# Token weights kept whole, kernel products four channels wide, in a long-convolution kernel with one routed token

## The chip, the cores and the metric

The kernel runs on one core of a Trainium2 chip. The metric is the device time of one execution in microseconds (us). The core has five engines with queues of their own: TensorE (PE; its weight loads, PEld, overlap its products), VectorE (DVE), ScalarE (ACT), GpSimd (POOL) and SyncE (SP), which only issues transfers. Each engine takes its instructions strictly in the order in which they were written into its queue, and an instruction that has to wait holds up all that stand behind it.

## The reference, cut to what matters

```
x  = A_u                                     # 1 x 2048 x 512, bf16
xn = layernorm(x)
# A: a long convolution of each of the 512 channels
K[d, l] = Re( sum_n C[d,n] * exp(dt[d] * A[d,n] * l) * dt[d] * B[d,n] )      # n < 128, l < 2048
y  = irfft( rfft(xn padded to 4096) * rfft(K padded to 4096) )[:2048]
s  = y + xn * Dskip
# B: one token of 2048 goes through a gated feed-forward network
r   = xn @ w_r;  idx = argmax(r)
f   = (silu(xn[idx] @ w_gate) * (xn[idx] @ w_up)) @ w_down                   # 512 -> 1376 -> 512
xb  = xn;  xb[idx] += f * sigmoid(r[idx])
out = x + s * silu(xb)
```

## The kernel before, in words

The whole program is one graph of operations. A builder writes them down with the buffers that they read and write; the table `ORDER` then gives, for each engine, the numbers of its operations in the order in which they are put into its queue, and the waits between engines follow from the buffers. Buffers share memory by fixed addresses (`R1`, `R2`, `RE`, `RS_` and so on), so that a write into a buffer also waits for all readers of what lay there. Nearly every instruction is recorded by one of a few helpers, which is why the profile shows few lines: `tt` (L596, products and sums of two tensors on DVE), `act` (L591), `evac` (PSUM to memory, L624 on ACT, L625 on DVE), `mm` (L642, products on PE), `dma` (L659).

The stages, in the order of the data:

- *Norm.* The input X comes in four loads into `X0`. DVE takes statistics and normalises 16 blocks into `XN`, together with ACT. 16 transfers regroup XN into `XZN`; four more write XN to a scratch in device memory, `scr_g`.
- *Router.* 64 products of XZN with `MR` (the weights w_r spread out) give the scores of all tokens. DVE and PE take turns over small pieces (`LRT`, `SML`) until the address of the largest stands in `SMI`. POOL gathers that token's row from `scr_g` by an indirect transfer into `GX`.
- *Input transform.* `useq1`: 64 products of XZN with a Fourier matrix, evicted into `AU` (16 evictions of 1024 columns, on ACT). `useq2`: 128 products of AU with `F2A` and `F2B`, evicted into `BIG` (16 evictions), the spectrum of the input. BIG lies over X0 and XN, 32 KB of each partition.
- *Convolution kernel.* It is made in four quarters of 128 channels (`h`, `s`, in the profile's order 00, 01, 10, 11). `exps` and `sines` make 32 lags of exponentials (`E`) and sines (`SN`) for 256 channels on ACT; `cols` turns them into real and imaginary columns on DVE; `rows_` makes 20 further powers `GG` by complex products `cmul` on DVE with multipliers `MB` and scratch `TT`. `kgen_mm` multiplies both: for each channel and part one product of 128x32 by 128x20, four channels beside each other in the PE array, evicted to `KE` and spread into `KX` by a few more products.
- *Spectrum.* `spec`: 160 products of KX with the transform `FD` per quarter, evicted into `KF`; DVE multiplies them into BIG. `inv_a` multiplies BIG (and a swapped copy, made by transfers) by the first inverse matrix, evicted into `CC`.
- *Token.* The network's weights come in 27 pieces through a ring of four buffers `WRING`, each a transfer that POOL issues when the piece before it has been used. The product of gate and up and the down product are spread among the kernel products on PE. The result is added to the token's row (`GRW`), and an indirect transfer scatters it back into `scr_g`.
- *End.* `G0` (printed as G) is loaded from `scr_g`, over the memory of SN, and goes through silu on ACT in four pieces. `fin`: CC times the last inverse matrix `FB`, five blocks for each half of the channels; DVE multiplies with G into `TB`, partly after an ACT eviction `YB`, and adds X in `XR`, which is stored.

The last lines of the builder set the numbering of the operations: `exps(0)`, `sines(0)`, `rows_`, `cols`, `kgen_mm(0, 0)`, and so on to `spec(1, 1)`, `inv_a(1, 1)`, `fin(1)`.

Of the kernel before, what the change touches and what calls it, by code (L numbers as in the profile page):

```python
# [16 lines left out]
KB = 1024  # L17
# [300 lines left out]
ROWS = [0, 4, 256, 260, 512, 516, 768, 772, 1024, 1280, 1536, 1792, 2, 6, 258, 262, 1, 5, 3, 7]  # L318
# [9 lines left out]
def tables():  # L328
# [33 lines left out]
    for q in range(2):  # L362
# [17 lines left out]
        580 564 562 565 689 767 770 332 695 701-702 779 704 797 781 783 782 794 809 800 815 789-790 812 792 818 881 884 890 896 822 834 902 826 835  # L380
        820 905 836-837 907 913 864 868-869 876 915 925 927 921 930 941 943 946 934 933 949-950""",
    vector="""
        295 294 149 147 157 155 150 148 144 146 143 152 151 145 99 96 98 104 101 107 109 158 156 154 100 106 108 103 153 39 159 97 171 160 105 161
        40 162 42 163 38 164 111 165 37 166 41 167 102 168 110 169 112 170 113 172 114 173 115 124 116 179 117 174 118 177 119 176 120 178 121 44
        122 175 123 93 125 95 126 94 129 132 131 130 133 127 66 68 59 64 61 60 63 69 62 67 77-78 80 83 70 65 71 84 74 89 85 92 72-73 436-437 90
        438-439 470 445 471 440 444 203 446-447 202 453 452 441 454 443 442 529 448-449 455 450 460 472 461 451 462 456-457 463 459 496 465 469 458
        473 468 474 476 464 475 467 466 530 532 531 477 535 533 536 534 495 205 498 206 497 207 504 500 499 209 502 501 503 507 506 211 505 212 512
        213 511 214 513 508 514 510 520 519 509 522 515-516 216 617 517 619 523 527 518 218 524 219 525 220 521 221 618 528 620-621 526 626 357 627
        223 358 224 628-629 623 635 634 622 637 625 624 636 631 630 643 632-633 642 638-639 644 640 645 641 650-651 705 646 706-707 647 708-709 648
        714-715 227 717 716 649 723 711 662 722 710 724 713 725 712 664 655 652 719 718 731 720-721 668 727 730 665 674 732-733 726 671 728-729 734  # L390
        739 735 738 683 737 736 677 680 750 755 753 758 653 685 654 658 656 659 657 764 756 765 743 762 744 768 745 691 771 759 331 329-330 328 746
# [17 lines left out]
def build(nc, A_u, A_A_re, A_A_im, A_B_re, A_B_im, A_C_re, A_C_im, A_log_dt, A_Dskip,  # L409
# [51 lines left out]
    with g.ctx:  # L461
# [425 lines left out]
        for m4 in range(16):  # L887
            useq1(m4)
# [361 lines left out]
```

## Time and profile before

| | |
|---|---|
| runs shown | 194.26, 191.87, 194.05 us; median 194.05 |
| the profiled execution | 194.93 us; its span on the core 193.1 us |
| granted TensorE clock, mean | 0.867 |
| busy of the span | PE 136.7 us (71%), DVE 153.1 (79%), ACT 131.8 (68%), POOL 24.9 (13%) |
| instructions | PE 2960 products, DVE 385, ACT 258, POOL 37 |
| moved | 31.64 MB in 24849 packets |

The page gives the busy share of each engine in 40 slices of the span, the granted clock of PE (10 tenths are full speed), the waits, and the chain of work that ended last, followed back from the last instruction to whatever released it. A timeline row has start, length, engine, line, instruction, what it writes and reads, shapes, and a count where equal neighbours are put together; in brackets, the idle time before it and what ended it. In a product's row stand first the columns that are moved through the array and then the stationary operand, and the second shape is that of what is moved.

### The profile page before, as it was taken

To read this page: it belongs to the slowest core of one execution; us is meant where nothing else is said; L and a number is where in the kernel's file an instruction comes from. 1 tells how busy PE (TensorE), PEld (TensorE's weight loads), DVE (VectorE), ACT (ScalarE), POOL (GpSimd) and SP (SyncE) were. 2 spreads that over 40 slices of the span, in tenths; PEclk is the share of its full clock that TensorE was granted. 3 is DMA by queue.
4 is the path that set the end of the run, shared out by engine and by line. 5 is a ranking of instruction groups with operands and counts; after the bars stand their busy time and mean duration, and the time that the engine had idled before them with its cause. 6 is when DMAs were issued, how large, how long until landed. Compare 5 with 4: busy or idle time off the path is not lost.

```text
span 193.1 us, 6819 instructions
## 1 busy us (share of the span) xinstructions
PE 136.7 (71%) x2960; PEld 117.9 (61%) x2960; DVE 153.1 (79%) x385; ACT 131.8 (68%) x258; POOL 24.9 (13%) x37
## 2 busy tenths in 40 slices
PE   0110800096887998992899995799999999969741
PEld 0000700094555674871899995798999899958520
DVE  0979999999999899995899999187526429569972
ACT  0799999999999989987768973123224352599321
POOL 6000000000000000691134040033130100000000
PEclk9999999999669559998599999555699999987975
DMA  5996016690000009899955999058255294914465
GB/s 153 392 380 249 2 54 207 228 384 0 0 0 0 5 3 312 196 316 334 300 135 147 224 201 244 15 160 216 65 157 142 55 377 88 340 35 100 97 124 117
DMA packets 24849, 31.64 MB, mean 164 GB/s; under 512 B 11028, under 2 KB 19348, under 8 KB 24180
## 3 DMA queue, kind: packets, MB, share of 16 engines
q1 hardware_dynamic: 19438, 23.14, 40.9%
q10 hardware_dynamic: 3894, 3.84, 7.4%
q0 software_dynamic: 1488, 4.23, 7.1%
q8 instruction: 23, 0.38, 0.8%
q14 instruction: 6, 0.05, 0.1%
HBM read 20.72 MB, written 4.20 MB: 129 GB/s over the span
## 4 chain that ended last, share of the span: by engine, by line
PE 33%; DVE 30%; DMA 20%; issue 9%; ACT 4%; POOL 1%; SPq 1%; POOLq 0%; DVEq 0%
PE PB L642 33%; DMA GX<-scr_g,SMI 7%; DMA X<-in_A_u_dram 5%; DVE TT L596 5%; DMA scr_g<-GRW,SMI 4%; DMA G<-scr_g 4%; DVE SL L596 3%; DVE GG L596 3%; DVE ST L791 3%; DVE XN L815 2%; DVE MB L596 2%; DVE SN L596 2%; DVE E L596 2%; DVE TB L596 2%; ACT YB L591 1%
## 5 line engine op out<-in xcount | busy, mean ns | idle before, releaser
L642 PE MATMUL PB<-KX,FD 128*128 128x128 bf16 x640 | 42.3, 229 | 0.0
L642 PEld LDWEIGHTS PB<-KX,FD 128*128 128x128 bf16 x640 | 39.6, 104 | 0.5 <-issue 0.2
L596 DVE TENSOR_TENSOR BIG<-BIG,KF 128x1024 bf16<-128x1024 bf16 x32 | 21.5, 688 | 14.5 <-ACT KF L624 14.4
L596 DVE TENSOR_TENSOR TT<-GG,MB 128x512 bf16<-128x512 bf16 (+2 forms) x64 | 27.9, 470 | 0.0
L624 ACT ACTIVATE KF<-PB 128x512 bf16<-128x512 f32 x23 | 13.7, 594 | 20.3 <-PE PB L642 19.2
L642 PE MATMUL PB<-CB,BIG 128*128 128x128 bf16 x256 | 23.3, 257 | 2.1 <-ACT CC L624 1.7
L642 PEld LDWEIGHTS PB<-CB,BIG 128*128 128x128 bf16 x256 | 20.8, 155 | 3.0 <-DVE BIG L596 2.0
L642 PE MATMUL PB<-GG,SN 128*32 128x20 bf16 x512 | 18.8, 220 | 3.4 <-issue 3.4
L642 PEld LDWEIGHTS PB<-GG,SN 128*32 128x32 bf16 x512 | 18.0, 170 | 3.5 <-issue 3.5
L591 ACT ACTIVATE E<-AR 128x256 bf16<-128x256 f32 x62 | 20.0, 403 | 0.0
L642 PE MATMUL PB<-GG,E 128*32 128x20 bf16 x512 | 19.1, 223 | 0.4 <-DVE E L596 0.4
L642 PEld LDWEIGHTS PB<-GG,E 128*32 128x32 bf16 x512 | 17.5, 167 | 2.8 <-issue 1.8
L882 POOL DMA_INDIRECT GX<-scr_g,SMI x1 | 8.1, 8071 | 74.8 <-DVE GG L596 74.8
L596 DVE TENSOR_TENSOR GG<-TT 128x256 bf16<-128x256 bf16 (+2 forms) x66 | 17.6, 305 | 0.0
L624 ACT ACTIVATE BIG<-PB 128x1024 bf16<-128x1024 f32 x16 | 15.8, 1016 | 1.4 <-PE PB L642 1.3
L642 PE MATMUL PB<-MR,XZN 128*128 128x64 bf16 x64 | 5.9, 275 | 14.7 <-DMA XZN<-XN 14.7
L624 ACT ACTIVATE AU<-PB 128x1024 bf16<-128x1024 f32 x16 | 15.4, 1035 | 0.6 <-PE PB L642 0.6
L642 PE MATMUL PB<-CB,XZN 128*128 128x256 bf16 x64 | 13.4, 360 | 2.6 <-ACT AU L624 2.6
L642 PEld LDWEIGHTS PB<-MR,XZN 128*128 128x128 bf16 x64 | 5.8, 205 | 15.0 <-DMA XZN<-XN 15.0
L791 DVE BATCH_NORM_STATS2 ST<-X 128x6 f32<-128x512 bf16 x16 | 10.2, 675 | 5.7 <-DMA X<-in_A_u_dram 5.7
L624 ACT ACTIVATE CC<-PB 128x1024 bf16<-128x1024 f32 (+1 forms) x11 | 9.5, 878 | 6.7 <-PE PB L642 6.7
L642 PEld LDWEIGHTS PB<-CB,XZN 128*128 128x128 bf16 x64 | 8.8, 182 | 6.8 <-ACT AU L624 6.3
(128 smaller groups left out, 250.1 us busy)
## 6 DMA issues: line engine op xcount, KB each, us to landing
FD<-c_fd SPq DMA_DIRECT2D x4, 1280.0 KB, 9.5
XZN<-XN SPq DMA_DIRECT2D x16, 128.0 KB, 2.1
scr_g<-XN SPq DMA_DIRECT2D x4, 512.0 KB, 3.4
XR<-in_A_u_dram SPq DMA_DIRECT2D x4, 512.0 KB, 9.8
FB<-c_fb SPq DMA_DIRECT2D x1, 2048.0 KB, 9.1
G<-scr_g SPq DMA_DIRECT2D x2, 1024.0 KB, 8.9
BIG<-BIG ACTq DMA_DIRECT2D x3, 512.0 KB, 5.8
WRING<-in_B_w_down_dram POOLq DMA_DIRECT2D x10, 128.0 KB, 2.8
```

The costliest lines, as they stand in the source:

```text
L591: g.op(AC, lambda e: e.activation(out=out.ap, in_=in_.ap, func=func, **kw), w=[out], r=r, cost=extra + cost(AC, out, 0.834) - (20 if in_.b ...
L596: g.op(eng, lambda e: e.tensor_tensor(out=out.ap, in0=a.ap, in1=b.ap, op=op), w=[out], r=[a, b], cost=cost(eng, out, rate))
L624: g.op(AC, lambda e: e.activation(out=out.ap, in_=in_.ap, func=ACT.Copy), w=[out], r=[in_], cost=cost(AC, out, 0.834) - 20, alt=(DV, lambd ...
L642: ins = e.matmul(o_.ap, lhsT=l_.ap, rhs=r_.ap, start=st, stop=sp, **kw)
L791: g.op(DV, lambda e, b=b: e.bn_stats(ST6(ST6.a[b]).ap, X0(X0.a[b]).ap), w=[ST6(ST6.a[b])], r=[X0(X0.a[b])], cost=593)
L815: lambda e, ov=ov, iv=iv, mv_=mv_, rv=rv: e.tensor_scalar(out=ov.ap, in0=iv.ap, scalar1=mv_.ap, scalar2=rv.ap, op0=ALU.subtract, op1=ALU.m ...
L882: g.op(PO, lambda e: e.indirect_dma_start(out=GX(None, 0, 8).ap, out_offset=None, in_=rows, in_offset=bass.IndirectOffsetOnAxis(ap=SMI(Non ...
```

## The change

1. *Weights.* The ring and its 27 transfers on POOL's queue are gone. Six transfers on SP load all of w_gate, w_up and w_down at once: `WGA` (w_gate and a quarter of w_up) into the memory of X0, `WGB` into that of MR, `WGC` into the old ring, `WDN` (all of w_down) into the memory of XN. Since BIG lies over X0 and XN, every eviction of useq2 has to wait for the network's last product. The network's code stands ahead of useq1.
2. *Kernel products.* E, SN and CO are laid out by quarter, channel group and lag, GG with both parts side by side. One product takes four channels, 128 stationary columns (4 channels x 32 lags) by 80 moved ones (4 x 20); of its 4 x 4 blocks only the diagonal ones are used. A quarter has 64 of them in three pieces, each evicted to `K4`. Before it had 256 column-packed ones and one eviction.
3. *Complex products.* `cmul` makes all four partial products in one instruction where the source allows it, so three instructions instead of four. `cols` has three instructions instead of nine, and the chain that makes the multipliers uses double-width ones.
4. *Order.* A new `ORDER`, another list `ROWS` of the powers, three YB buffers, four PSUM bank pairs in the second `fin`, larger stores.

The core of the diff:

```diff
-ROWS = [0, 4, 256, 260, 512, 516, 768, 772, 1024, 1280, 1536, 1792, 2, 6, 258, 262, 1, 5, 3, 7]
+ROWS = [0, 256, 512, 768, 4, 260, 516, 772, 1024, 1280, 1536, 1792, 1, 5, 2, 6, 3, 7, 258, 262]
-        E = g.buf("E", RE, [32, 256], BF16)
-        GG = g.buf("GG", RG, [2, 20, 256], BF16)
+        E = g.buf("E", RE, [2, 4, 32, 32], BF16)
+        GG = g.buf("GG", RG, [20, 2, 256], BF16)
-        WRING = [g.buf(f"WRING{i}", RWR + 1536 * i, [768], BF16) for i in range(NWR)]
+        WGA = g.buf("WGA", R2, [5, 1376], BF16)
+        WGB = g.buf("WGB", R1 + 32 * KB, [2, 1376], BF16)
+        WGC = g.buf("WGC", RWR + 2560, [1376], BF16)
+        WDN = g.buf("WDN", R2 + 16 * KB, [11, 512], BF16)
...
+        load(WGC(), _dma_rows(B_w_up, 384 * FF, [[FF, 128], [1, FF]]), 128 * FF * 2, eng=None)
+        load(WGA(WGA.a[0:4]), rows_of(B_w_gate, 0, 4), 512 * FF * 2, eng=None)
+        load(WGA(WGA.a[4]), _dma_rows(B_w_up, 0, [[FF, 128], [1, FF]]), 128 * FF * 2, eng=None)
+        load(WGB(), rows_of(B_w_up, 1, 2), 256 * FF * 2, eng=None)
+        load(WDN(WDN.a[0:10]), _dma_rows(B_w_down, 0, [[512, 128], [65536, 10], [1, 512]]), 1280 * 1024, eng=None)
+        load(WDN(WDN.a[10], 0, 96), _dma_rows(B_w_down, 655360, [[512, 96], [1, 512]]), 96 * 1024, eng=None)
...
             sc = TT[si[0] % 2]
-            tt(DV, sc(t[0]), src, MB(bc(mr, (2, n, w))), ALU.mult)
-            tt(DV, sc(t[1]), src, MB(bc(mi, (2, n, w))), ALU.mult)
-            tt(DV, dst_r, sc(t[0, 0]), sc(t[1, 1]), ALU.subtract)
-            tt(DV, dst_i, sc(t[0, 1]), sc(t[1, 0]), ALU.add)
+            if n == 1 or src.strides[0] == 2 * src.strides[1]:
+                sv = np.lib.stride_tricks.as_strided(src, shape=(2 * n, w), strides=(src.strides[1], src.strides[2]))
+                tt(DV, sc(t.reshape(2, 2 * n, w)), GG(bc(sv[None], (2, 2 * n, w))), MB(bc(m[:, None], (2, 2 * n, w))), ALU.mult)
+            else:
+                for k in range(2):
+                    tt(DV, sc(t[k]), GG(src), MB(bc(m[k], (n, 2, w))), ALU.mult)
+            tt(DV, GG(dst[:, 0]), sc(t[0, :, 0]), sc(t[1, :, 1]), ALU.subtract)
+            tt(DV, GG(dst[:, 1]), sc(t[0, :, 1]), sc(t[1, :, 0]), ALU.add)
...
-                    for j in range(4):
-                        ch = 128 * s + 32 * j + c
-                        lst.append((bank(bank.a[o_:o_ + 20], 32 * j, 32), (E, SN)[ri]((E, SN)[ri].a[:, ch]), GG(GG.a[ri, :, ch]), ri == 0, ri == 1, (0, 32 * j)))
+            for c0, n in ((0, 6), (12, 6), (24, 4)):
+                for c in range(2 * n):
+                    for ri in range(2):
+                        gv = GG.a[:, ri, 128 * s:128 * s + 128].reshape(20, 32, 4)[:, c0 + c]
+                        lst.append((bank(bank.a[o_:o_ + 80]), (E, SN)[ri]((E, SN)[ri].a[s].reshape(128, 32)[:, c0 + c]), GG(gv), ri == 0, ri == 1, None))
+                mm(lst, 63)
+                evac(K4(K4.a.reshape(80, 32)[:, c0:c0 + 2 * n].reshape(80, 2, n)), PP[0](PP[0].a.reshape(2, 512)[:, :80 * n].reshape(2, n, 80).transpose(2, 0, 1)))
...
-                pr = PP[3 * (kb % 2) if h else 0]
+                pr = PP[(0, 3, 2, 1, 0)[kb] if h else 0]
-                    y_ = YB[kb % 2]
+                    y_ = YB[kb % 3]
```

Where the router's end stands on DVE. Before, it lies behind the third quarter's first complex products; the index SMI is row 188 of DVE's queue, with the products of the powers (GG, TT) around it:

```order
182 L596 TENSOR_TENSOR GG<-TT_109 128x2x128
183 L596 TENSOR_TENSOR TT_108<-GG,MB 128x512
184 L603 TENSOR_SCALAR SMB<-SML 64x1
185 L596 TENSOR_TENSOR TT_108<-GG,MB 128x512
186 L596 TENSOR_TENSOR SML<-PB,CF 8x1
187 L606 CAST SML<-SMB 64x1
188 L606 CAST SMI<-SML 8x1
189 L596 TENSOR_TENSOR GG<-TT_108 128x2x128 x2
```

In the changed kernel the same instructions on DVE, ahead of the first column instructions of SN and E:

```order
105 L611 TENSOR_REDUCE SML<-LRT 64x1
106 L598 TENSOR_TENSOR GG<-TT_92 128x2x128
107 L598 TENSOR_TENSOR GG<-TT_91 128x4x128
108 L598 TENSOR_TENSOR SML<-PB,CF 8x1
109 L598 TENSOR_TENSOR GG<-TT_91 128x4x128
110 L608 CAST SMI<-SML 8x1
111 L598 TENSOR_TENSOR TT_92<-GG,MB 128x1024
112 L605 TENSOR_SCALAR SN<-SN 128x4x480
```

SMI has moved from row 188 to row 110, ahead of the work on SN and E and of the third quarter's powers.

On PE, in the changed kernel, between the input transform's first products (CB,XZN) and its second ones (AU,F2A) stand the products of the gathered row (GX) and all of the network's gate and up products:

```order
15 L644 MATMUL PB<-CB,XZN 128x256 x24
16 L644 MATMUL PB<-CB,GX 64x4 x2
17 L644 MATMUL PB<-CB,XZN 128x256 x4
18 L644 MATMUL PB<-SMB,CB 128x32
19 L644 MATMUL PB<-SMB,WGA 128x1 x10
20 L644 MATMUL PB<-SMB,WGA 96x1
...
36 L644 MATMUL PB<-SMB,WGC 96x1
37 L644 MATMUL PB<-SMB,CB 128x32
38 L644 MATMUL PB<-AU,F2A 128x4x64 x16
39 L644 MATMUL PB<-GG,E 128x80
```

Before, at that place on PE, the first products ran through and the kernel products followed them; GX's two products came only after all second transforms:

```order
4 L642 MATMUL PB<-CB,XZN 128x256 x8
5 L642 MATMUL PB<-LRT,CF 64x32
6 L642 MATMUL PB<-CB,XZN 128x256 x56
7 L642 MATMUL PB<-GG,E 32x20 x4
8 L642 MATMUL PB<-GG,SN 32x20 x4
```

So the wait for GX has moved to behind 52 of the 64 first products, and 12 of these, the network and all that follows stand behind it.

The silus of G on ACT, among the evictions KF and CC. Before:

```order
144 L624 ACTIVATE CC<-PB 128x128x8
145 L591 ACTIVATE G_132<-G_132 128x2048
146 L624 ACTIVATE KF_123<-PB 128x512
147 L624 ACTIVATE CC<-PB 128x128x8
148 L591 ACTIVATE G_132<-G_132 128x2048
149 L624 ACTIVATE CC<-PB 128x128x4
150 L624 ACTIVATE CC<-PB 128x128x8
151 L591 ACTIVATE G_132<-G_132 128x2048 x2
```

In the changed kernel:

```order
143 L626 ACTIVATE KX_103<-PB 128x640
144 L626 ACTIVATE KF_106<-PB 128x512
145 L593 ACT_TABLE_LOAD
146 L593 ACTIVATE G_114<-G_114 128x2048 x4
147 L626 ACTIVATE KF_107<-PB 128x512
148 L626 ACTIVATE CC<-PB 128x128x8
```

All four silus now stand together, right behind the first spectrum eviction of the last quarter.

More of the change, by code (lines that the diff above doesn't have):

```diff
@@ new lines, in build @@
+        g.stage = "ffn"
+        todo = [(wi, dc) for wi in range(2) for dc in range(4)]
+        for k, (wi, dc) in enumerate(todo):
+            wb, wa = wv(wi, dc)
+            lst = [(fv(0, 32), CB(cb("IDB")), gu, True, False, None)] if k == 0 else []
+            for fc in range(11):
+                Mf = 128 if fc < 10 else 96
+                lst.append((fv(16 * wi + fc, 1, 0, Mf), wb(wa[128 * fc:128 * fc + Mf]), SMB(SMB.a[16 + dc:17 + dc]), False, False, None))
+            if k == 7:
+                lst.append((fv(0, 32), CB(cb("IDB")), gu, False, True, None))
+            mm(lst, 30)
@@ new lines, in build @@
+        for wi in range(2):
+            cp(DV, SMB(SMB.a[32 + 16 * wi:42 + 16 * wi]), fv(16 * wi, 10))
+            cp(DV, SMB(SMB.a[42 + 16 * wi:43 + 16 * wi], 0, 96), fv(10 + 16 * wi, 1, 0, 96))
+        act(SMB(SMB.a[64:75]), SMB(SMB.a[32:43]), ACT.Silu, table="silu")
+        tt(DV, SMB(SMB.a[80:91]), SMB(SMB.a[64:75]), SMB(SMB.a[48:59]), ALU.mult)
+        lst = [(fv(32, 4), CB(cb("IDB")), SMB(SMB.a[104:108]), True, False, None)]
+        for fc in range(11):
+            Kf = 128 if fc < 10 else 96
+            for dc in range(4):
+                lst.append((fv(32 + dc, 1), WDN(WDN.a[fc, 128 * dc:128 * dc + 128], 0, Kf), SMB(SMB.a[80 + fc:81 + fc], 0, Kf), False, False, None))
+            if fc in (3, 7):
+                mm(lst, 32)
+                lst = []
@@ new lines, in build @@
+        lst.append((fv(32, 4), CB(cb("IDB")), SMB(SMB.a[104:108]), False, True, None))
+        mm(lst, 32)
+        act(sml(6, 0, 64), sml(2, 0, 64), ACT.Tanh, scale=0.5, table="silu")
+        ts(DV, SMB(SMB.a[100:101], 0, 64), sml(6, 0, 64), 0.5, 0.5, ALU.mult, ALU.add)
+        cp(DV, sml(7, 0, 64), SMB(SMB.a[100:101], 0, 64))
+        cp(DV, SMB(SMB.a[108:112]), fv(32, 4))
+        mm([(fv(40, 128, 0, 4), SMB(SMB.a[108:112]), CB(cb("IDB")), True, True, None)], 100)
+        four = lambda t: t(None, 0, 4)
@@ new lines, in build @@
+        cp(DV, four(UPD), fv(40, 128, 0, 4))
+        ts(DV, four(UPD), four(UPD), sml(7, 0, 4), None, ALU.mult)
+        dma(GRW(None, 0, 8).ap, bass.AP(tensor=UPD.handle, offset=0, ap=[[UPD.row, 4], [64, 2], [1, 64]]), 1024, w=[GRW(None, 0, 8)], r=[UPD(None, 0, 4)])
+        tt(DV, GRW(None, 0, 8), GRW(None, 0, 8), GX(None, 0, 8), ALU.add)
+        g.op(PO, lambda e: e.indirect_dma_start(out=rows, out_offset=bass.IndirectOffsetOnAxis(ap=SMI(None, 0, 8).ap, axis=0), in_=GRW(None, 0, 8).ap, in_offset=None),
+             r=[GRW(None, 0, 8), SMI(None, 0, 8)], cost=950, dma=16 * KB, tokr=[f"scrg{a}" for a in range(4)], tokw=["row"])
@@ L1143, in build @@
-        dma(GRW(None, 0, 8).ap, bass.AP(tensor=UPD.handle, offset=0, ap=[[UPD.row, 4], [64, 2], [1, 64]]), 1024, w=[GRW(None, 0, 8)], r=[UPD(None, 0, 4)])
-        tt(DV, GRW(None, 0, 8), GRW(None, 0, 8), GX(None, 0, 8), ALU.add)
-        g.op(PO, lambda e: e.indirect_dma_start(out=rows, out_offset=bass.IndirectOffsetOnAxis(ap=SMI(None, 0, 8).ap, axis=0), in_=GRW(None, 0, 8).ap, in_offset=None),
-             r=[GRW(None, 0, 8), SMI(None, 0, 8)], cost=950, dma=16 * KB, tokr=[f"scrg{a}" for a in range(4)], tokw=["row"])
+                if kb in SEND[h]:
+                    q0, qn = SEND[h][kb]
+                    for p_ in range(4):
+                        store(_dma_rows(out, 16384 * (p_ // 2) + 512 * q0 + 256 * (p_ % 2) + 128 * h, [[32768, 32], [512, qn], [1, 128]]), XR(XR.a[q0:q0 + qn, 128 * h:128 * h + 128], 32 * p_, 32), 32 * 256 * qn, eng=None)
```

273 lines of the change are left out of this document (107 added, 166 removed), and 4 rows, old and new, of the table scalar.

## The prediction

> **What bounds the kernel now.** I read the busy digits of the page first: 40 slices of 4.83 us for each engine, the granted TensorE clock, and the DMA engines.
>
> ```profile
> PE   0110800096887998992899995799999999969741
> DVE  0979999999999899995899999187526429569972
> ACT  0799999999999989987768973123224352599321
> PEclk9999999999669559998599999555699999987975
> DMA  5996016690000009899955999058255294914465
> ```
>
> DVE is full from 10 to about 118 us, PE from about 63 to 182. ACT leaves its full stretch at about 108. So there are two regimes, a vector half and a TensorE half, and neither engine works in the other's. The stretches in numbers (columns: length; PE, PEld, DVE, ACT, POOL busy with counts; clock; DMA share; GB/s):
>
> ```profile
> 11.86:46.30 34.44, 12.39 (x92) 10.85 (x92) 34.44 (x106) 33.80 (x87) 0.00 (x0) 1.00 0.50 187
> 46.30:62.20 15.90, 11.83 (x62) 7.68 (x62) 15.81 (x42) 15.34 (x20) 0.00 (x0) 0.79 0.00 0
> 62.20:92.40 30.20, 24.70 (x692) 18.14 (x692) 26.35 (x95) 26.84 (x52) 8.66 (x3) 0.80 0.64 195
> 92.40:118.60 26.20, 26.13 (x519) 25.27 (x520) 25.55 (x57) 20.74 (x52) 6.45 (x12) 0.91 0.90 199
> 118.60:138.80 20.20, 17.02 (x322) 15.72 (x321) 12.78 (x21) 4.37 (x7) 4.26 (x8) 0.58 0.51 137
> 138.80:152.50 13.70, 13.69 (x425) 13.23 (x424) 6.85 (x13) 4.11 (x6) 1.67 (x4) 1.00 0.40 107
> 152.50:168.00 15.50, 15.41 (x271) 14.25 (x271) 8.39 (x16) 7.17 (x11) 0.85 (x1) 1.00 0.73 243
> 168.00:180.00 12.00, 9.71 (x306) 8.82 (x303) 9.37 (x12) 11.16 (x10) 0.00 (x0) 0.86 0.32 86
> 180.00:193.10 13.10, 5.20 (x296) 3.62 (x294) 8.16 (x14) 2.64 (x3) 0.00 (x0) 0.73 0.60 123
> ```
>
> The chain that ended last names what each stretch waits for (start, length, what):
>
> ```profile
> 62.18 11.31 PE PB L642 x299
> ...
> 78.96 13.44 DMA GX<-scr_g,SMI
> 92.39 0.04 issue
> 92.44 26.13 PE PB L642 x518
> 118.57 3.21 issue
> 121.78 18.59 PE PB L642 x382
> ...
> 142.36 9.78 issue
> 152.14 0.28 POOLq L292
> 152.43 8.11 DMA scr_g<-GRW,SMI
> 160.55 6.96 DMA G<-scr_g
> ...
> 189.92 0.42 DVE XR L596
> ```
>
> After 118.6 the vector engines wait for TensorE, which loses time twice: it stands 3.21 us in "issue", and from 122 to 138.8 it is granted about half the clock. Then the token's path closes the chain: its row can be scattered only at 152.43, the gate G returns at 167.5, and the silus of G fall where the last products need them.
>
> **The front end.** Prices (start, length, instruction, idle before):
>
> ```profile
> 26.43 10.32 SPq L659 DMA_DIRECT2D XZN<-XN  x16
> 38.27 5.89 PE L642 MATMUL PB<-MR,XZN 128*128 128x64 bf16 x64 [14.66 <-DMA XZN<-XN]
> 78.50 0.14 DVE L606 CAST SMI<-SML 8x1 int32<-8x1 f32 x1
> 78.96 8.07 POOL L882 DMA_INDIRECT GX<-scr_g,SMI  x1 [74.84 <-DVE GG L596]
> 64.80 1.01 ACT L624 ACTIVATE BIG<-PB 128x1024 bf16<-128x1024 f32 x1
> 115.18 1.22 DVE L596 TENSOR_TENSOR E<-E,CO 128x1024 bf16<-128x1024 bf16 x2
> 134.97 1.23 DVE L596 TENSOR_TENSOR E<-E,CO 128x2048 bf16<-128x2048 bf16 x1
> ```
>
> A 1024-element bf16 product takes 0.6 us, a 2048-element one 1.15: merging instructions saves only some 0.05 each. Adding up DVE's instructions in both orders at these prices, DVE has 2.6 us less ahead of the last XN, 25 us less ahead of SMI, 0.6 us more ahead of the last column instruction of the third quarter, and 3 us less ahead of that of the fourth. So XN ends 2.6 us sooner. SP issues 14 XZN transfers where it issued 16 of 0.645 us, the other two go through ACT, so it keeps up and the router's 64 matmuls start near 35.6. SMI comes at about 51 (bounds 48, if few of the row products ahead of it delay it, and 58).
>
> The gather then takes POOL 8.07 us, plus what it took from there to landing: 13.44 in all, under the DMA share of 0.64. The scatter's 8.11 is the lower bound. I take 12.1, so GX lands near 63.1 (59 to 71). Here the change adds its **new wait**. PE's queue reaches the gather after 52 of the 64 first-transform matmuls, near 58; behind it stand the other 12, all gate and up products, all second transforms. ACT's AU evictions and then DVE run dry near 59.5. Each microsecond that GX lands later is one for all three. I charge 3.6 us (0 to 12).
>
> The big weight loads need SP to issue six transfers behind XZN, into a stretch in which the DMA share is 0.00 (46.3 to 62.2): they are hidden there. What they cost if that cover is gone: as the new second wait, BIG overlays WGA and WDN, and so no second-transform eviction can begin before the down product. After the gather come 88 gate and up and 44 down products and a silu, about 8.7 us together, so the first BIG eviction moves from 64.8 to about 72. ACT has column and exponential work ahead of it meanwhile, and DVE its row products, so I price the delay at nothing beyond the 3.6; if their queues drain, up to 7.
>
> Before, DVE went from the last XN (31.0) to the third quarter's last E (116.4) in 85.4 us, of which it idled 3.85 + 0.65 in the two windows from 62.2 to 118.6: 80.9 of work. In the new order that piece is 3.2 longer (0.6 more in all, 2.6 less ahead of it): 84.1. I drop the 4.5 of idle time and put the 3.6 in its place: 28.4 + 84.1 + 3.6 = 116.1. **Gain 0.3**: the vector half is as long as before, with the FFN now inside it.
>
> **Kernel matmuls.** A group of four column-packed products, and larger ones with a strided or plain stationary operand:
>
> ```profile
> 62.34 0.23 PE L642 MATMUL PB<-GG,E 128*32 128x20 bf16 x4
> 62.41 0.24 PE L642 MATMUL PB<-GG,SN 128*32 128x20 bf16 x4
> ...
> 103.48 0.59 PE L642 MATMUL PB<-SMB,WRING 128*128 128x1 bf16 x17
> 103.93 1.28 PE L642 MATMUL PB<-KX,FD 128*128 128x128 bf16 x20
> ...
> 155.37 1.21 PE L642 MATMUL PB<-CB,BIG 128*128 128x128 bf16 x16
> 156.42 3.51 PE L642 MATMUL PB<-KX,FD 128*128 128x128 bf16 x60
> ```
>
> Four packed products start every 67 ns: 1024 cost 17.1 us. The new 256 load 128 columns at a stride of 32 elements, as CB,BIG does: 16 start in 1.05 us, 65.6 ns each, so 256 cost 16.8. **Even.** The bounds: 26.5 ns (17 WRING products in 0.45 us, plain loads, one column moved) and 92 (MR,XZN: 64 in 5.89, stride 64), so −10 to +6.8 us over four quarters; half of it lies after mm10 on the path. A quarter now has three evictions instead of one:
>
> ```profile
> L624 ACT ACTIVATE KE<-PB 128x640 bf16<-128x640 f32 x4 | 2.8, 702 | 8.5 <-PE PB L642 8.5
> ```
>
> At 702 ns for 640 columns, two of 960 and one of 640 cost about 2.5, 1.8 more a quarter; ACT is idle from 118 on, so nothing for the last two; in the first two, 3.6 us of ACT beside a DVE-bound stretch.
>
> [...]
>
> **TensorE half.** From the third quarter's last E to the end of the fourth quarter's products took 116.4 to 152.4 = 36.0 us before. In the new order that stretch holds 128 kernel products (8.4), 88 of CB,BIG (5.8), 80 of KX,FD at 58.5 ns (4.7) and 1.5 of small ones: 20.4. The FFN's products are gone from it, 60 KX,FD move behind it, the fetch stall and the half clock are for now left out. **Gain 15.6.** The end, 136.5, needs the fourth quarter's columns from DVE; by its sum they come near 126 (before 136.2), so they do not bind.
>
> Behind it to the first final product: 240 KX,FD (14.0), 48 CB,BIG (3.1) and 1.6, so 18.7; before 15.1. **Loss 3.6**, the moved products.
>
> The tail from there to the last XR was 167.5 to 190.3 = 22.8. Four silus of G stand in it:
>
> ```profile
> 167.53 1.92 ACT L591 ACTIVATE G<-G 128x2048 bf16<-128x2048 bf16 x1 [1.77 <-DMA G<-scr_g]
> ```
>
> 7.3 us of an ACT that was busy 11.16 of 12. Now the row is scattered long before, and G's load waits only for SN's buffer, free after the last kernel product at 136.5; landing takes about 8 (G 7.0 on the chain), so the silus run to 152, beside spectrum products. Then the first half of the tail is DVE's 9.4, and the last half, with three YB buffers and four bank pairs in turn, DVE's five products and sums of 5.2 with one YB eviction behind: 6.5. Together 15.9. **Gain 6.9.** What is late next is the spectrum's ACT evictions behind the four silus: if DVE does not take them, up to 7.
>
> Sum: 194.93 (the span 193.1 and 1.83 around it) − 0.3 − 15.6 + 3.6 − 6.9 = 175.7. To that I add clock and fetch losses. Before, 16.8 us at a clock of 0.50 to 0.53 cost at most 8.2, and the stall 3.2. The change removes no cause that I can name, and its waits are different; I put 4.3 of the 11.4 back, over a third: **180**. The profiled run is 0.9 above the median of 194.05, less than my rounding.
>
> [...]
>
> **The rivals.**
> - *The losses come along* (0.20). The order is right, but the half clock and the stall return in full, 7.1 over my 4.3: 187, from 185 to 190. For it: the clock dropped in four separate places. Against: PE has fewer distinct groups.
> - *Everything fits* (0.09). GX lands by 59.5, the clock stays full: 175.7 − 3.6 = 172 (169 to 174).
> - *No change* (0.06). The change doesn't do what it says: BIG's wait for the down product puts ACT 4 us behind, new stationary loads cost 92 ns (+3.4 on the path), G's load is held up behind SP's 4 BIG transfers so the silus stay in the tail (+6.9): 180 + 14 = 194, from 190 to 198.
> - *Slower* (0.05). PE at half clock from mm10 on. It then has 20.4 + 18.7 + 9 = 48 us of work, and 48 more at 0.50 would give 176 + 48 = 224; it decides from 22 us of extra wall time, that is, a good 40 us at half clock. Before, 16.8 us of such clock is the longest seen. I put 198 to 212 there.
>
> **How the numbers follow.** Likeliest 180 with 0.60, own range 174 to 185. With a bound of 2% (190.2 and 197.9; about what the measurement can tell): faster holds 0.60 + 0.20 + 0.09, less a little of the second: 0.86; same 0.09; slower 0.05. The range runs from 169 to 190 and leaves out the last two rivals.
>
> **What would show it.** Right: GX issued near 51 and PE waiting for it 3 to 5 us; the first BIG eviction near 72; 128-column kernel products every 66 ns; E of the fourth quarter done near 126; the scatter long before 100 and the silus of G over before 155. Wrong: kernel products near 92 ns, GX landing after 68, DVE idling between 70 and 116, or TensorE at a granted clock near 0.5 for more than 10 us after 116.

## The result and the profile after

| | before | after |
|---|---|---|
| median of the runs | 193.78 us (191.87 to 194.26) | 180.24 us (179.82 to 181.75) |
| ratio, 95% interval | | 0.933 (0.925 to 0.942) |
| the profiled execution; its span | 194.93; 193.1 us | 181.75; 179.9 us |
| granted TensorE clock, mean | 0.867 | 0.970 |
| busy: PE, DVE, ACT, POOL | 136.7, 153.1, 131.8, 24.9 us | 129.2, 149.4, 139.8, 12.4 us |
| products on PE, instructions on DVE | 2960, 385 | 2192, 329 |

The forecast was 180.0 us (169 to 190). The median lies 0.2 above it, the profiled execution, on which the sum is made, 1.8. Some terms of the sum were off by more than that, with both signs. Some executions of a kernel are slower than the rest (the kernel before took 190.65 to 197.56 us in 16 of them); the medians count them, the ratios do not, and the profiled execution of the kernel before (194.93) is one of them.

First the busy digits of the kernel after, 40 slices of 4.5 us (a row for each engine, then the granted clock of TensorE):

```profile
PE   0100035296968399999985789999999999999240
DVE  0899999999999488999999899899643599679831
ACT  0799889999999377999999859998645399964430
PEclk9999999999999999999998899999999999999965
```

Three things stand out against the rows of before. The full stretch of PE in the second half is shorter. The 5s in the row of the clock between 116 and 140 us are gone. And PE, DVE and ACT dip together in the fourteenth slice (3, 4 and 3), from 58.5 to 63 us: that is the new wait for the gathered row.

The same stretches in numbers, cut at the prediction's own marks: the router's first product, the first BIG eviction, the third quarter's last E, the fourth quarter's last kernel product, the first final product, the last XR (start and end, length; PE, PEld, DVE, ACT, POOL busy with counts; clock; DMA share; GB/s):

```profile
34.82:60.00 25.18, 20.96 (x128) 14.62 (x128) 25.00 (x57) 24.35 (x43) 7.87 (x1) 1.00 0.62 219
60.00:72.88 12.88, 10.65 (x193) 9.40 (x194) 8.83 (x25) 8.24 (x19) 1.12 (x1) 1.00 0.01 2
72.88:117.90 45.02, 40.85 (x621) 35.52 (x620) 43.09 (x96) 41.96 (x86) 2.13 (x2) 0.96 0.67 187
117.90:137.70 19.80, 19.80 (x322) 19.06 (x320) 13.86 (x18) 13.58 (x19) 0.72 (x1) 1.00 0.81 165
137.70:156.30 18.60, 18.60 (x315) 17.39 (x314) 14.36 (x26) 14.26 (x14) 0.00 (x0) 1.00 0.65 228
156.30:176.07 19.77, 13.14 (x602) 11.35 (x600) 14.79 (x22) 9.60 (x11) 0.00 (x0) 0.91 0.41 84
```

Up to 117.9 DVE is the full engine, apart from 60 to 72.9, where it idles 4 us. From 117.9 to 156.3 PE has no idle time at all, at full clock: 38.4 us of pure product time where before 51.1 (116.4 to 167.5) passed, with a stall of 3.21 us and 16.8 us at a clock of 0.50 to 0.53 among them.

Then the chain that ended last (start, length, what):

```profile
52.13 10.06 DMA GX<-scr_g,SMI
...
92.51 11.52 DMA FD<-c_fd
104.16 59.77 PE PB L644 x1165
...
166.29 0.81 issue
...
168.38 2.99 issue
```

The gather stands in it with 10.06 us, and at the end PE stands twice in "issue" in the middle of the final products, 3.8 us together. The load of FD that the chain names at 92.5 made PE wait for 2.3 us only, while DVE went on; in the profile of the second control below the chain runs through DVE's products there. PE's waits (what waited, on what: us in total, times, longest):

```profile
PE PB L644 <- DMA GX<-scr_g,SMI: 2.8, 1, 2.8
PE PB L644 <- DMA FD<-c_fd: 2.3, 2, 1.7
```

The four products of CB,XZN next behind the row's two in the queue do not read GX; they, too, started only at 62.38, behind the 2.8 us.

The marks of the prediction, with the rows of the kernel after that carry them (timeline):

```profile
34.82 5.87 PE L644 MATMUL PB<-MR,XZN 128*128 128x64 bf16 x64 [4.36 <-DMA XZN<-XN]
115.70 2.16 DVE L598 TENSOR_TENSOR E<-E,CO 128x3840 bf16<-128x3840 bf16 x1
125.56 2.15 DVE L598 TENSOR_TENSOR E<-E,CO 128x3840 bf16<-128x3840 bf16 x1
146.19 7.32 ACT L593 ACTIVATE G<-G 128x2048 bf16<-128x2048 bf16 x4
175.65 0.42 DVE L598 TENSOR_TENSOR XR<-TB,XR 128x512 bf16<-128x512 bf16 x1
```

| mark | before | predicted | after |
|---|---|---|---|
| router's 64 products start | 38.27 | 35.6 | 34.82 |
| index SMI; row GX landed | 78.5; 92.4 | 51; 63.1 | 51.7; 62.2 |
| first BIG eviction | 64.8 | 72 | 72.9 |
| third quarter's last E | 116.4 | 116.1 | 117.9 |
| fourth quarter's last E | 136.2 | 126 | 127.7 |
| fourth quarter's last kernel product | 152.4 | 136.5 | 137.7 |
| first final product | 167.5 | 155.2 | 156.3 |
| silus of G over | 177.6 | 152 | 153.5 |
| last XR | 190.3 | 171.1; 175.4 with the 4.3 put back | 176.1 |

### The profile page after: what moved, and what is told of

The parts are those of the page before. It is cut to its first block, busy times and chain, and to the rows that moved or that the text cites. A ratio compares the mean times of both kernels' runs of the same rounds, so it can differ in the third digit from the quotient of the medians.

```text
span 179.9 us, 5187 instructions
## 1 busy us (share of the span) xinstructions
PE 129.2 (72%) x2192; PEld 111.7 (62%) x2192; DVE 149.4 (83%) x329; ACT 139.8 (78%) x259; POOL 12.4 (7%) x8
## 4 chain that ended last, share of the span: by engine, by line
PE 53%; DVE 19%; DMA 15%; SPq 5%; issue 3%; ACT 3%; DVEq 0%
PE PB L644 53%; DMA FD<-c_fd 6%; DMA GX<-scr_g,SMI 6%; SPq L661 5%; DMA X<-in_A_u_dram 3%; DVE XN L809 3%; DVE MB L598 2%; DVE TT L598 2%; DVE ST L785 2%; DVE SLA L598 2%; DVE MR L598 1%; ACT BIG L626 1%; DVE SLA L616 1%; ACT K L626 1%; ACT YB L593 1%
## 5 line engine op out<-in xcount | busy, mean ns | idle before, releaser
L598 DVE TENSOR_TENSOR TT<-GG,MB 128x1024 bf16<-128x1024 bf16 (+2 forms) x36 | 24.9, 710 | 0.1
L593 ACT ACTIVATE E<-AR 128x256 bf16<-128x256 f32 x62 | 19.8, 402 | 0.0
L644 PE MATMUL PB<-CB,BIG 128*128 128x128 bf16 x256 | 19.0, 229 | 0.0
L644 PE MATMUL PB<-GG,E 128*128 128x80 bf16 x128 | 17.4, 241 | 0.0
L644 PE MATMUL PB<-GG,SN 128*128 128x80 bf16 x128 | 17.4, 240 | 0.0
L644 PEld LDWEIGHTS PB<-GG,E 128*128 128x128 bf16 x128 | 16.2, 164 | 1.4 <-issue 0.6
L644 PE MATMUL PB<-DPF,WC 128*128 128x128 f32 x16 | 4.1, 441 | 17.1 <-DVE WC L598 17.1
L644 PEld LDWEIGHTS PB<-GG,SN 128*128 128x128 bf16 x128 | 16.4, 165 | 0.0
L626 ACT ACTIVATE CC<-PB 128x1024 bf16<-128x1024 f32 (+1 forms) x16 | 13.7, 876 | 2.9 <-PE PB L644 2.8
L626 ACT ACTIVATE K<-PB 128x960 bf16<-128x960 f32 (+1 forms) x11 | 9.9, 898 | 6.3 <-PE PB L644 6.2
L644 PEld LDWEIGHTS PB<-DPF,WC 128*128 128x128 f32 x16 | 3.6, 327 | 17.7 <-DVE WC L598 17.7
L626 ACT ACTIVATE BIG<-PB 128x1024 bf16<-128x1024 f32 x14 | 13.8, 1020 | 0.0
## 6 DMA issues: line engine op xcount, KB each, us to landing
FD<-c_fd SPq DMA_DIRECT2D x4, 1280.0 KB, 10.1
```

Source lines behind the costliest of these rows:

```text
L593: g.op(AC, lambda e: e.activation(out=out.ap, in_=in_.ap, func=func, **kw), w=[out], r=r, cost=extra + cost(AC, out, 0.834) - (20 if in_.b ...
L598: g.op(eng, lambda e: e.tensor_tensor(out=out.ap, in0=a.ap, in1=b.ap, op=op), w=[out], r=[a, b], cost=cost(eng, out, rate))
L626: g.op(AC, lambda e: e.activation(out=out.ap, in_=in_.ap, func=ACT.Copy), w=[out], r=[in_], cost=cost(AC, out, 0.834) - 20, alt=(DV, lambd ...
L644: ins = e.matmul(o_.ap, lhsT=l_.ap, rhs=r_.ap, start=st, stop=sp, **kw)
```

## The experiments

Three terms needed a test, since a forecast can be right by terms that cancel: the wait for GX, the price of the kernel products, and the tail. All kernels are the changed one with the edit shown, except the last. Times are medians with their range.

### What does the gather wait for?

In the kernel after, the gather and VectorE beside it (timelines: start, length, instruction, idle before):

```profile
52.13 8.99 POOL L876 DMA_INDIRECT GX<-scr_g,SMI  x1 [51.09 <-DVE SMI L608]
```
```profile
51.73 0.67 DVE L598 TENSOR_TENSOR TT<-GG,MB 128x1024 bf16<-128x1024 bf16 x1
52.34 0.64 DVE L605 TENSOR_SCALAR SN<-SN 128x1920 bf16<-128x1920 bf16 x1
...
58.02 0.14 DVE L605 TENSOR_SCALAR SMB<-SML 64x1 bf16<-64x1 f32 x1
58.08 2.13 DVE L598 TENSOR_TENSOR SN<-SN,E 128x3840 bf16<-128x3840 bf16 x1
62.49 0.16 DVE L608 CAST SMB<-PB 128x4 bf16<-128x4 f32 x1 [2.28 <-PE PB L644]
```

The gather's span ends at 61.1, 0.9 after VectorE ran dry at 60.2. It isn't the transfer engines that hold it there: between 58.3 and 61.1 their share is 0.00. The prediction had taken 8 us of GpSimd for the gather's own work, so that GX lands a fixed time behind the index, and charged one microsecond for each that it lands later. The first test moves the index, and with it the gather, 6.3 us later; the unaltered kernel ran beside it as the control.

> The changed kernel once more, unaltered, beside the kernel before: 180.2 us, 0.930 to 0.935 of before. It says how far runs that share a chip differ from the runs shown, and the experiments of this group are read against it. If its profile shows TensorE idle in 'issue' near 166 and 168 us again (0.8 and 3.0 us), that stall belongs to the program; if it comes at another place or not at all, it is chance.

Measured: 180.33 us (179.54 to 182.16), ratio to before 0.943 (0.927 to 0.958). The control repeats.

**A later index.** The operation 211, the cast to SMI, goes behind seven instructions of VectorE, two of them column products of 2.14 us:

```diff
- ... 210 400 211 401 458 402-403 459 411 460 241 412 ...
+ ... 210 400 401 458 402-403 459 411 460 211 241 412 ...
```

> One number moved in the vector queue: the cast that makes the token index SMI comes behind six column and power instructions of 6.3 us in all. Theory (the wait for the gathered row stands in front of TensorE, ScalarE and VectorE, each microsecond costs one): GX is issued near 58, lands near 68.5, TensorE idles 9 us before it, and the time rises by 6.3 to about 186.5. Rival (VectorE or ScalarE have slack behind it): the column work was done meanwhile, 0 to 3 us more. Second rival (a long idle gap of TensorE halves its granted clock): more than 8 us, with a granted clock near 0.5 behind the gap.

Measured: 180.73 us (179.66 to 181.56), ratio 0.944 (0.932 to 0.956). The theory fell. The trace of this kernel shows why:

```profile
58.56 2.71 POOL L876 DMA_INDIRECT GX<-scr_g,SMI  x1 [57.52 <-DVE SMB L605]
```

It starts 6.4 us later and ends at 61.27, where it ended before, and the row lands at 62.5 instead of 62.2. Most of its 8.99 us had been waiting, not work: in both kernels it ends 0.9 us after the same VectorE product of SN and E is over (at 60.21 and 60.36), whenever it starts.

**No wait for the row.** The two products that read GX read a constant instead, so that the row's content is left out of the token's path and nothing on PE waits for it:

```diff
-        mm([(mv(130, 4, 64 * i, 64), GX(None, 0, 8), CB(...), ...
+        mm([(mv(130, 4, 64 * i, 64), CB(cb("IDB")[0:64], 0, 8), CB(...), ...
```

> The two products that bring the gathered row to the network read a constant in place of GX, so the row that the network sees is wrong and nothing waits for the gather. Theory: the gaps of 2.8 us on TensorE, 3.0 on ScalarE and 2.3 on VectorE near 60 us close, the weights have all landed by then, and the time falls by 2.3 to about 178. Rival (another wait stands right behind it, the weights or the down product ahead of BIG): less than 1 us.

Measured: 177.62 us (176.56 to 181.45), ratio 0.924 (0.907 to 0.941), 2.7 below its control. So the wait is worth about what it measures on PE and DVE (2.8 and 2.3 us). The trace of this kernel shows more. The gather, which nothing on PE waits for now, and VectorE at its end:

```profile
52.12 8.99 POOL L876 DMA_INDIRECT GX<-scr_g,SMI  x1 [51.07 <-DVE SMI L608]
```
```profile
58.06 2.14 DVE L598 TENSOR_TENSOR SN<-SN,E 128x3840 bf16<-128x3840 bf16 x1
60.13 0.14 DVE L608 CAST SMB<-PB 128x4 bf16<-128x4 f32 x1
60.20 0.13 DVE L608 CAST SML<-SMB 64x1 f32<-64x1 bf16 x1
60.26 2.14 DVE L598 TENSOR_TENSOR E<-E,CO 128x3840 bf16<-128x3840 bf16 x1
```

VectorE does not run dry here: two casts of 0.1 us follow the long product, and then the next one. The gather ends at 61.11 all the same, 0.9 after the product of SN and E. So it does not need VectorE to stop.

**Let GpSimd go first.** If it is VectorE's work that holds the gather up, a pause of VectorE right behind the index should bring it through. GpSimd writes one element behind the gather, and VectorE's next instruction waits for that:

```diff
-        351 212 506 249""",
+        351 212 838 506 249""",
+        memset(PO, sml(50, 0, 1), 0.0)
+        g.ops[401].preds.add(838)
```

> The gather was issued 6.3 us later in the experiment before and yet landed at the same time: its span on GpSimd shrank from 8.99 to 2.71 us, and both ended 0.9 us after the same VectorE product of SN and E. So here VectorE's next instruction behind the index cast waits for a one-element memset that GpSimd does right after the gather's span; nothing else changes. Theory (GpSimd cannot get through the gather while VectorE runs one two-input instruction on the other, and needs 0.9 us once it pauses): the gather's span is about 1 us, VectorE idles about 1.5 us near 52, GX lands near 54.5, the three waits near 60 are gone, and the time is 1 us lower, near 179. Rival (the gather is slow by itself or by the weight loads around it): its span stays near 9 us, VectorE idles all of it, and the time rises by 6 to 7.

Measured: 179.20 us (178.60 to 184.59), ratio 0.933 (0.926 to 0.940). The gather and the instruction that was held up, in this kernel:

```profile
52.15 1.02 POOL L876 DMA_INDIRECT GX<-scr_g,SMI  x1 [51.11 <-DVE SMI L608]
```
```profile
53.31 0.69 DVE L598 TENSOR_TENSOR TT<-GG,MB 128x1024 bf16<-128x1024 bf16 x1 [1.48 <-POOL SML L630]
```

8.99 us have become 1.02. VectorE paid 1.48 for it. The row itself lands only 4 us earlier, near 58.2 (6.1 us from start to landing, where the kernel after has 10.1). The load of w_down, which SP issues, runs at the same time: in the kernel after the share of the transfer engines is 1.08 from 55 to 57 and 0.04 from 58.0 to 58.3, and in the slice from 54 to 58.5 us the pages of both kernels show 0.8. That the row waits for this load is argued, not shown. PE reaches the row's products at 58.77 and does not wait.

**Short copies instead of a pause.** Six copies of one column (64x1), two behind each of three instructions after the index, to give GpSimd openings without a wait:

```diff
- ... 400 211 401 458 402-403 459 411 460 241 412 ...
+ ... 400 211 401 838-839 458 840-841 402-403 842-843 459 411 460 241 412 ...
+        for k in range(6):
+            cp(DV, sml(50 + k, 0, 64), CF(CF.a[m0:m0 + 1], 0, 64))
```

> The changed kernel with six copies of one column (0.07 us each) on VectorE, two behind each of the three instructions that follow the index cast. If a short one-input instruction is pause enough for GpSimd, the gather ends within 3 us of its start, GX lands near 56 and the time falls by about 2.3 to 178; if it takes a real pause of VectorE, the gather ends at 61 as before and the time rises by 0.4.

Measured: 177.71 us (175.66 to 179.28), ratio 0.931 (0.923 to 0.938), which is not clearly apart from the handshake: the ratios are 0.931 and 0.933. As the unaltered kernel had not run beside these two, it ran once more side by side with the short copies:

> The changed kernel with the six short copies of one column on VectorE, once more, beside the changed kernel unaltered on the same chip. If the short copies let the gather through, its row lands near 59 instead of 62.2 and the time is 2.5 us (1.5 to 3.5) below that of the unaltered kernel. If the difference seen before lay between chips, the two agree within 1 us.

> The changed kernel, unaltered, on the chip of the other three runs: 180.2 us (179.5 to 181.5), and the two stalls of TensorE in the tail again, some 3.8 us together.

Measured: 177.65 us (176.84 to 181.35), ratio 0.923 (0.915 to 0.930), against 180.95 us (179.12 to 181.64), ratio 0.940 (0.932 to 0.947): 3.3 us less, and **a version that beats both kernels**. PE reaches the row's products at 58.8 and does not wait for it. The gather with the copies, and the stretch from 58 to 66 us with them and without (same columns as above):

```profile
51.95 1.88 POOL L876 DMA_INDIRECT GX<-scr_g,SMI  x1 [50.90 <-DVE SMI L608]
```
```profile
58.00:66.00 8.00, 6.98 (x118) 5.96 (x120) 7.53 (x19) 6.83 (x13) 0.00 (x0) 0.71 0.01 2
```
```profile
58.00:66.00 8.00, 4.49 (x52) 3.88 (x53) 5.52 (x7) 3.86 (x5) 2.88 (x1) 0.72 0.00 0
```

In these 8 us PE does 2.5, DVE 2.0 and ACT 3.0 us more work: the wait that the change had added is gone, for six instructions of 0.1 us. Which of the six it takes was not tried.

### Are the kernel products worth the same?

The prediction counted a group of four packed products and one wide product at the same 66 ns, and left out what they do to others. Here the wide product is split into the packed form again, first with each of the four moving all 80 columns:

```diff
-   lst.append((bank(bank.a[o_:o_ + 80]), (E, SN)[ri](... .a[s].reshape(128, 32)[:, c0 + c]), GG(gv), ..., None))
+   for j in range(4):
+       lst.append((bank(bank.a[o_:o_ + 80], 32 * j, 32), (E, SN)[ri](... .a[s, j][:, c0 + c]), GG(gv), ..., (0, 32 * j)))
```

> The changed kernel with each kernel product of 128 stationary columns split into four column-packed ones of 32, side by side in the array, each moving the same 80 columns; results are the same, TensorE has 768 more products and weight loads. Theory (a packed group of four and a wide product both start every 66 ns; the gain lies in order and waits): within 1 us of 180. Rival (the gain comes from fewer TensorE instructions, through fetch stalls and the granted clock): stalls and half clock come back, 186 to 190.

Measured: 198.17 us (197.07 to 198.40), ratio 1.032 (1.019 to 1.045): **18 us more**, and slower than the kernel before. Both theories missed. To see whether the fourfold moved data does it, each packed product then moved its own 20 columns, as before the change:

```diff
+       lst.append((bank(... .reshape(20, 4)[:, j], 32 * j, 32), (E, SN)[ri](... .a[s, j][:, c0 + c]), GG(gv[:, j]), ..., (0, 32 * j)))
```

> Four column-packed products again in place of each wide one, but now each moves only its own channel's 20 columns, as the kernel before did. The packed ones that moved 80 columns each cost 18 us, and instructions of VectorE and ScalarE that ran beside them took up to five times as long. Theory A (that comes from four operands of 80 columns read at once; the packing itself is even with the wide product): within 2 us of 180, no slow VectorE instructions. Theory B (the wide product is itself a gain, by fewer instructions and fetches): 184 or more.

Measured: 197.16 us (196.36 to 198.35), ratio 1.028 (1.022 to 1.035). It is not the moved data: theory A fell, and of theory B the bound held. The groups show where the time is (busy us, mean ns of one). In the kernel after:

```profile
L644 PE MATMUL PB<-GG,E 128*128 128x80 bf16 x128 | 17.4, 241 | 0.0
L626 ACT ACTIVATE BIG<-PB 128x1024 bf16<-128x1024 f32 x14 | 13.8, 1020 | 0.0
L598 DVE TENSOR_TENSOR GG<-TT 128x256 bf16<-128x256 bf16 x42 | 10.4, 281 | 0.0
```

With four packed products of 20 columns each:

```profile
L644 PE MATMUL PB<-GG,E 128*32 128x20 bf16 x512 | 21.6, 268 | 5.8 <-issue 4.4 <-DVE GG L598 1.0
L626 ACT ACTIVATE BIG<-PB 128x1024 bf16<-128x1024 f32 x14 | 18.5, 1376 | 0.0
L598 DVE TENSOR_TENSOR GG<-TT 128x256 bf16<-128x256 bf16 x42 | 12.8, 354 | 0.0
```

The same instructions of DVE and ACT take longer, with no wait in front of them. Where they run beside packed products the difference is large:

```profile
69.59 2.05 DVE L598 TENSOR_TENSOR GG<-TT 128x256 bf16<-128x256 bf16 x2
```

The row is two instructions, which need 0.5 us together elsewhere. In all DVE is busy 161.4 us instead of 149.4, in a kernel whose first 118 us hang on it, and PE has a stall of 4.4 us in front of packed products: 12.0 and 4.4 come near the 17 us lost, though no run separates the two. What stays open is why the kernel before, with packed products too, does not show it:

```profile
L596 DVE TENSOR_TENSOR GG<-TT 128x256 bf16<-128x256 bf16 x42 | 10.5, 281 | 0.0
```

Its stationary columns lay 256 elements apart instead of 32, and no run here changed that stride. So these two runs say that the new layout needs the wide product; they do not say that the wide product made the change faster than the kernel before.

### What is the tail made of?

**Late silus.** The four silus of G are put back among the last evictions of CC:

```diff
- ... 692 712 734-735 737 736 781 722 790 787 726 720 793 724 797 ...
+ ... 692 712 781 722 734 790 787 726 720 735 793 724 737 736 797 ...
```

> The changed kernel, but the four silus of G stand among the last evictions of CC, as they did before the change. If they are what made the tail before 22.8 us long, ScalarE has 7.3 us more in a stretch in which it is the releaser of TensorE, and the time rises by the 6.9 us of the prediction's tail term, less what the two stalls of TensorE hide: 186 (184.5 to 187.5). If VectorE takes the evictions over or TensorE's stalls bound the tail anyway, under 2 us: 180 to 182.

Measured: 185.31 us (184.66 to 188.10), ratio 0.963 (0.951 to 0.975), 4.4 above its control. PE's waits in the kernel with late silus (what waited, on what: us in total, times, longest):

```profile
PE PB L644 <- ACT CC L626: 4.9, 3, 2.5
PE PB L644 <- issue: 1.4, 1, 1.4
```

In the kernel after no wait for CC is left, and "issue" has 3.8 us in two pieces. So PE waits 4.9 us for ACT, and 2.4 of the stalls are gone at the same time. 4.4 and 2.4 make 6.8, near the prediction's 6.9, if the stalls went because PE was late anyway; that is argued. Measured are the 4.4.

**Smaller stores.** Do the stalls come from the stores, which the DMA engines carry beside the instructions (23 packets, 0.33 MB in the kernel after)? The stores of the first half's five blocks write a sixteenth; the rest of these outputs is left out:

```diff
-                    q0, qn = SEND[h][kb]
+                    q0, qn = SEND[h][kb] if h else (SEND[h][kb][0], 1)
```

> The stores of the first half of the channels write one row where they wrote 16 (the rest of that half is not written), so almost no store traffic runs while the last products are issued. In both profiles of the changed kernel TensorE stands about 3.8 us in 'issue' among the last 256 small products (10 ns each). Theory (its instruction fetch queues behind the stores): the stalls go, 3 to 4 us less, near 177. Rival (products of 10 ns use up instructions faster than they can be fetched, stores or not): the stalls stay, less than 1 us.

Measured: 181.06 us (180.84 to 183.69), ratio 0.946 (0.938 to 0.953). The stalls stay:

```profile
PE PB L644 <- issue: 3.9, 3, 2.4
```

From 161 to 174.5 us, three slices of the page, the DMA share is 0, 1 and 3 tenths here, and in the same three of the kernel after 5, 6 and 4, with 0.99 during its longest stall; the longest stall takes 2.4 and 3.0 us. What causes the stalls is open. In the trace of the kernel after they divide the 256 final products of the second half into pieces of 101, 128 and 27. The middle piece, with as many weight loads, has 128 products again in the chains of both controls and of the second kernel with the short copies.

**Fewer products of the network.** To price what left the TensorE half, the kernel before with one product for each of the 27 pieces instead of 132 in all; the products of the other rows are left out:

```diff
-                    for fc in range(f0, f0 + fn_):
+                    for fc in range(f0, f0 + 1):
-            for dc in range(4):
+            for dc in range(1):
```

> The kernel before, but with one product for each piece of the network's weights (27 of 132, all transfers kept; the products of the other rows are left out). Where TensorE bounds the stretch from 116 to 152 us, the some 60 products that go there at 52 ns are worth 3.2 us, and up to 5 if part of them ran at half clock: 190 (188.5 to 191). If their time only turns into the wait for the ring's transfers or for the fourth quarter's columns, under 1 us: 193 to 194. If they also carry the stall and the half clock, over 8: below 186.

Measured: 190.07 us (187.67 to 192.86), ratio 0.986 (0.979 to 0.992) to the 193.33 of the kernel before beside it: 3.3 less by the medians, 2.8 (1.6 to 4.0) by the ratio. The 66 products in the TensorE half are busy 3.5 us, and 51 of them are left out here, so the size is about what was expected. The window there:

```profile
118.00:152.00 34.00, 29.52 (x771) 26.80 (x763) 20.53 (x37) 10.03 (x16) 6.79 (x12) 0.90 0.56 136
```

The clock is 0.90, so the loss of clock does not hang on these products alone. It is also higher than in the profile of before (0.58 for 20 of these us); part of the gain may be that, and one profile of each does not tell them apart.

## Why the prediction was right, and where its terms were off

| step | predicted | measured |
|---|---|---|
| vector half, to the third quarter's last E | -0.3 | +1.5 |
| stretch to the fourth quarter's last product | -15.6 (36.0 to 20.4) | -16.2 (19.8) |
| from there to the first final product | +3.6 | +3.5 |
| tail to the last XR | -6.9 | -3.0, with 3.8 of stalls in it |
| losses of clock and fetch, put back | +4.3 | in the row above |
| after the last XR | 0 | +1.1 |
| sum, from 194.93 | 180.0 | 181.8 |

- **The TensorE half** was the large term, and its size was right. The largest part that left is the spectrum's products, before and after (busy us, mean ns):

```profile
L642 PE MATMUL PB<-KX,FD 128*128 128x128 bf16 x167 | 12.0, 236 | 0.0
```
```profile
L644 PE MATMUL PB<-KX,FD 128*128 128x128 bf16 x83 | 5.1, 219 | 0.0
```

  By the prediction's prices the 84 fewer are 4.9 us; the network's 66 products (3.5) are gone too, and 8 of CB,BIG came in: some 8 us of products. By this estimate the other 8 of the 16.2 fall to the stall of 3.21 us and the half clock (0.50 to 0.53), which did not come back. The prediction calls that stall a fetch stall; the trace has it as "issue", and no run shows a fetch behind it. The prediction named no cause that the change removes, left both out of the stretch and put 4.3 of them back at the end. So for half of this term no step gave a reason: that the losses stayed away here, while 3.8 us of stalls turned up in the tail, is luck as far as the runs show.
- **The front end.** The router started 0.8 us sooner than forecast, the index came 0.7 later. DVE's work in the vector half was right: from the last XN at 27.6 to 117.9 are 90.3 us, of which DVE idled 6.2, so 84.1 of work, the predicted figure. The mis-sized term is the idle time, put at 3.6. The network's two waits took that alone, and smaller ones, most of them for PE and ACT, 2.6 more (DVE in the stretch: busy time, then its largest wait: us in total, times, longest):

```profile
28.00:117.90 89.90, 74.53 (x947) 61.32 (x947) 83.74 (x184) 81.16 (x162) 11.12 (x3) 0.98 0.56 173
```
```profile
DVE SMB L608 <- PE PB L644: 3.6, 2, 2.3
```

  The weight loads were hidden (no instruction in the list of waits waited for WGA, WGB, WGC or WDN), and DVE had no long gap between 72.9 and 117.9, as priced.
- **The new wait** had the right size for a wrong reason. GX landed 0.9 sooner than forecast, and the 3.6 charged for it compares with 2.8 on PE (just under the mark of 3 to 5), 3.6 on DVE and 2.7 to 3.3 us of time in the runs. But the landing was reckoned from the index, with GpSimd's 8 us taken for work. An index 6.3 us later moved the landing by 0.3 and the time by 0.4, no more than the runs scatter. The lower bound taken from the scatter, 8.11 us from start to landing, fell too: the late gather took 4.0, the one with the handshake 6.1.
- **"Even" kernel products.** On PE the count was right; the wide products start 60 to 70 ns apart, neither 26.5 nor 92:

```profile
136.88 0.23 PE L644 MATMUL PB<-GG,SN 128*128 128x80 bf16 x1
136.94 0.24 PE L644 MATMUL PB<-GG,E 128*128 128x80 bf16 x1
```

  That the form of the product would change other engines was in no step: with column-packed products the changed kernel was 17 and 18 us slower.
- **The tail.** Its mechanism was right: the scatter no longer holds G up, all four silus were over at 153.5, and put back they cost 4.4 net. Mis-sized is the tail's length, 15.9 for 19.8; 3.8 of the 3.9 are the two stalls, which the 4.3 for "clock and fetch losses" covered. That total came out, by luck: it was a share chosen of old losses, and the half clock, for which most of it was meant, was gone in the PE-bound stretch. Without the 4.3 the sum would have been some 6 us below the profiled execution.
- One mark failed: the scatter came at 116.1, not "long before 100", since the result's last addition stands late in DVE's queue. It cost nothing that shows: G's load waited for SN's memory until 137.7 anyway, as forecast.

```profile
116.07 2.54 POOL L931 DMA_INDIRECT scr_g<-GRW,SMI  x1 [26.28 <-DVE GRW L598]
```

- The 1.1 us more behind the last XR were in no term, and no run takes them apart.

Why the half clock of before is gone is not settled. In the kernel after, PE has no gap between 104 and 164 us, while before it fell to half clock behind a stall of 3.21. But a wait alone does not decide it. In the kernel after, a wait of 4.36 us ahead of the router's products was followed by 25 us at 1.00. From 58 to 66 us it stood at 1.00 with a wait of 2.8 for GX, the second control at 0.72 with one of 3.4, and the second kernel with the short copies at 0.71, where PE idled 1.0 us in all. Nor does the mean clock of an execution fix its time: two of the kernel before, with 0.868 and 0.924, both took 190.7 us. No run took a gap of PE away alone.

## What to carry to other kernels

A long span of an indirect transfer on GpSimd need not be work: look whether its end moves with its start or stays behind the same VectorE instruction, and if it stays, try a few tiny one-input instructions behind the one that releases it (six copies of 0.1 us here, and a span of 8.98 us became 1.88). Price a product not by its start-to-start time on PE alone: compare the mean of the other engines' groups, too, because a form that is even on PE can stretch what runs beside it (here ScalarE's mean eviction, from 1020 to 1376 ns). When a sum comes out right, test its terms: here +1.8 us in the vector half and +1.1 behind the last XR stood against -1.1 elsewhere, most of the gather's 8 us were waiting, and half of the largest term was a loss that went away without a known cause.

## What the runs showed of the hardware that was not expected

- **The gather on GpSimd starved behind VectorE.** It took 1.02 us with VectorE paused, 1.87 and 1.88 with short copies in between, 2.71 to 8.99 otherwise. In the kernel after, the wait lasted over nine VectorE instructions in a row, three of them with one input, and a single short one (0.14 us at 58.02) did not end it. It ended when VectorE ran dry (at 60.21, the gather at 61.12), and also behind two casts of 0.1 us with VectorE going on (61.11, in the kernel without the wait for the row). The scatter took 0.92 us in the kernel before, where VectorE stood idle from 152.1 to 154.6. In the kernel after it took 2.54 us from 116.07 and came through while VectorE went on without any short one-input instruction, so what ends the wait is open.
- **Beside packed products VectorE and ScalarE were slower**: with stationary columns 32 elements apart, two instructions of VectorE took 2.05 us instead of 0.5, and the mean eviction of ScalarE 1376 ns instead of 1020; with 256 apart, in the kernel before, neither shows (281 and 1016 ns). The cause is open.
- **PE's stalls in "issue"** come at nearly the same place and length in the profiles of the unaltered kernel (0.81 and 2.99, 1.09 and 2.71, 0.86 and 2.71 us), stay (3.9 us together, the longest 2.4) with the first half's stores reduced to a sixteenth, and are 1.4 us with the late silus, where PE waits 4.9 us for ACT.
